# A fused attention, mixing and feed-forward kernel: the feed-forward in 18 tiles of 256 tokens across batch borders instead of 16 tiles of 288

## The chip, the cores and the metric

The program runs on one core of a Trainium2 chip. The metric is the device time of one execution in microseconds (us); of several runs the median counts. The core has five engines that work side by side, each in the order of its own instruction list: TensorE (PE: matrix products; PEld is its weight load), VectorE (DVE), ScalarE (ACT), GpSimd (POOL) and SyncE (SP), which issues the DMAs. TensorE writes its products to PSUM, eight banks of 512 float32 values per partition.

## What is computed

For 8 batches of 576 tokens, with 8 heads of 64 channels:

```python
q_d, k_d, v_d = means of q, k, v over groups of 4 tokens
out_up = repeat(softmax(q_d k_d^T / 8) v_d, 4 tokens)
out_local = softmax(q k^T / 8, keys at a distance under 4) v
x = (out_up + out_local), heads side by side          # 8 x 576 x 512
u = x + (V^T U^T along the tokens) x                  # U: 576 x 32, V: 32 x 576
out = u + relu(u @ w_ch1) @ w_ch2                     # 512 -> 2048 -> 512
```

A pair of heads fills the 128 partitions, so a batch is 4 pairs (`hp` 0 to 3) and the attention is 32 pairs in all. U, V and the two weights come as float64.

## The kernel before

**Feed-forward.** It works on transposed tokens: partitions are channels, columns are tokens. A batch's 576 tokens are cut into two tiles of `TN` = 288, 16 tiles in all. One step is one tile and one of the 16 chunks `fc` of 128 hidden channels, 256 steps in all. `ffn1` (L878) multiplies four channel chunks of u with W1 into one PSUM tile `ps_h`; `ffn2` (L900), three steps later (`LAG`), multiplies the rectified chunk with W2 into four accumulators `acc`, one for each 128 output channels and each in a PSUM bank of its own. To keep precision every operand is split into a high and a low float32r part, and a product is three matmuls (high·high, high·low, low·high): 12 matmuls of 288 columns in `ffn1` and 12 in `ffn2`, with a weight load of 128 columns ahead of each. ACT makes the high part `hH` from `ps_h` (L895), DVE the low part `hL` (L896). At the end of a tile POOL adds uH and uL (L921), DVE adds the accumulator (L924), and a DMA stores 128 channels (L927).

**u.** A tile's u lies in `uH` and `uL` (two buffers each). A head pair of the attention is one of its four channel chunks, so a tile's first step needs all four pairs of its batch. `mix_part` (L816) makes it from the pair's attention output `x_s` in DRAM: `xL` and `Y` are loaded from it, PE multiplies with U (`ps_hu`, L848), then per tile with V (`ps_u`, L863); DVE adds (L866), ACT rounds to `uH` (L869), POOL subtracts for `uL` (L871). Batch 0 takes another way (`early_mix`).

**Attention of a pair.** The first five pairs (batch 0 and pair 0 of batch 1) use `early_global` and `local_blocks`. The others use `late_global` (scores `ps_b`, L719 and L726; transposes `ps_t`, L539; products `ps_a`, L552; result `od`, stored to `up_s`) and `local_attn`, where POOL makes five products `Pt` (L799) and DVE sums them (L804) into `acc`, which goes to `x_s` (L806).

**Weights.** W1 and W2 come in 16 chunks each. `convert` (L335) turns the raw float64 bits into float32 and the two parts: ACT L341, DVE L342, L344, L347 and L349, ACT L351, POOL L354. W2 has its place in SBUF only after the early attention's pool is given back (`late`, L969). The raw chunks and POOL's `Pt` share three buffers (tag `Pt`).

**Order.** Nothing is issued where it is written. Every piece of work is an `op` of a planner (`Plan`, L54) with an engine, an estimated duration, what it reads and writes, and a priority; a simulated run (L95) fixes the order in which each engine's instructions are issued. The attention has 10 times the pair's number as priority, the W2 conversions 20 to 35, and the feed-forward matmuls 1000 plus their step, so they fill what is left of PE. `PH` and `PF` (L222) are the planner's durations for `ffn1`'s 12 matmuls and for three of `ffn2`.

Of the kernel before, what the change touches and what calls it, by code (L numbers as in the profile page):

```python
# [11 lines left out]
F32 = mybir.dt.float32  # L12
# [189 lines left out]
def attn_mix_ffn_kernel(ctx: ExitStack, tc, q, kp, vp, qT, kT, v, U, Ub, V, w1, w2, mask, band, eye, pat, pool, vw, vn, ident, outT):  # L202
# [11 lines left out]
    TN = 288  # L214
    NT = S // TN
    R = V.shape[0] // 4
    MP, MJ = U.shape[0], U.shape[1] // R
    LAG = 3
# [3 lines left out]
    PH, PF = 1.587, 0.398  # L222
# [52 lines left out]
    ident_sb = const.tile([128, 128], F32, name="ident_sb")  # L275
# [15 lines left out]

    band_sb = early_pool.tile([128, NS * KL], BF16, name="band_sb")
# [40 lines left out]
    dma(lambda: nc.sync.dma_start(out=mask_sb, in_=mask), [], ["mask"], 35, 32)  # L333

# [72 lines left out]

    heads = [slice(hh * D, (hh + 1) * D) for hh in range(2)]
# [86 lines left out]
    def late_global(b, hp, up_s, prio):  # L495
# [39 lines left out]
        def t_mm():  # L535
            for hh in range(2):
                for c in range(2):
                    for a in range(2):
                        nc.tensor.transpose(view(pt[hh])[:, c, a * QH:(a + 1) * QH],  # L539
                                            Es[hh]()[:, a, c * QH:(c + 1) * QH], ident_sb[:QH, :QH])  # L540
        op(PE, 0.52, t_mm, ek + ["ident"], pt, prio)
# [13 lines left out]
        od = g([QH, 4, D], "od")  # L555
# [114 lines left out]
    def early_mix(b, hp, x, prio):  # L670
# [14 lines left out]
        for t in range(NT):  # L685
            pu = psum(ps_m, "ps_u", "m:x", 2)
            cuts = [(r, max(t * TN, 128 * r), min((t + 1) * TN, 128 * (r + 1))) for r in range(NS)]
            cuts = [x for x in cuts if x[1] < x[2]]

            def um(t=t, pu=pu, cuts=cuts):  # L690
                tsl = slice(t * TN, (t + 1) * TN)
                nc.tensor.matmul(pu()[:, :TN], stk(), Vst[:, tsl], start=True, stop=False)
                for r, c0, c1 in cuts:
                    nc.tensor.matmul(pu()[:, c0 - t * TN:c1 - t * TN], flat(r), ident_sb[:, c0 - 128 * r:c1 - 128 * r],
                                     start=False, stop=(r == cuts[-1][0]))
            op(PE, pw(prio) * 1.05, um, rd + [(stk, 0), (stk, 1), (stk, 2), "ident", "V0H", "V1H", "V0L", "V1L"], [pu], prio)
            uH, uL = u_of(b, t)
            act(TN, lambda uH=uH, pu=pu: nc.scalar.activation(uH()[:, hp, :], pu()[:, :TN], AF.Copy),
                [pu], [(uH, hp)], prio, 0.05)
            dve(TN, lambda uH=uH, uL=uL, pu=pu: nc.vector.tensor_tensor(  # L700
                out=uL()[:, hp, :], in0=pu()[:, :TN], in1=uH()[:, hp, :].bitcast(F32), op=ALU.subtract),
                [pu, (uH, hp)], [(uL, hp)], prio)
# [106 lines left out]
    u_bufs = {}  # L809

    def u_of(b, t):
        if (b, t) not in u_bufs:
            u_bufs[(b, t)] = (buf(ffn, [128, NDC, TN], F32R, "uH", bufs=2), buf(ffn, [128, NDC, TN], F32R, "uL", bufs=2))
        return u_bufs[(b, t)]

    def mix_part(b, hp, x_s, prio):  # L816
# [21 lines left out]
        dve(576, lambda: nc.vector.transpose(xT(), Y().rearrange("p a d -> p (a d)")), [Y], [(xT, t) for t in range(NT)], prio)  # L838
# [18 lines left out]
        for t in range(NT):  # L857
            tsl = slice(t * TN, (t + 1) * TN)
            pu = psum(ps_m, "ps_u", "m:x", 2)

            def um(tsl=tsl, pu=pu):
                lt = stk().rearrange("p h d -> p (h d)")
                nc.tensor.matmul(pu()[:, :TN], lt, Vst[:, tsl], start=True, stop=True)  # L863
            op(PE, 0.14, um, [(stk, 0), (stk, 1), (stk, 2), "V0H", "V1H", "V0L", "V1L"], [pu], prio)
            uf, ufk = (lambda tsl=tsl: xT()[:, tsl]), (xT, t)
            dve(TN, lambda pu=pu, uf=uf: nc.vector.tensor_tensor(  # L866
                out=uf(), in0=pu()[:, :TN], in1=uf(), op=ALU.add), [pu, ufk], [ufk], prio)
            uH, uL = u_of(b, t)
            act(TN, lambda uH=uH, uf=uf: nc.scalar.activation(uH()[:, hp, :], uf(), AF.Copy),  # L869
                [ufk], [(uH, hp)], prio, 0.1)  # L870
            pool_tt(TN, lambda uH=uH, uL=uL, uf=uf: nc.gpsimd.tensor_tensor(  # L871
                out=uL()[:, hp, :], in0=uf(), in1=uH()[:, hp, :].bitcast(F32), op=ALU.subtract),
                [ufk, (uH, hp)], [(uL, hp)], prio)
# [4 lines left out]
    def ffn1(s, i):  # L878
        b, t, fc = s
        uH, uL = u_of(b, t)  # L880
# [13 lines left out]
        hL = buf(ffn, [128, TN], F32R, "hL", bufs=3)  # L894
# [5 lines left out]
    def ffn2(s, i):  # L900
        b, t, fc = s
# [3 lines left out]
        ac = accs[(b, t)]  # L905

        for e in range(NDC):
            def mm(e=e):
                es = slice(e * 128, (e + 1) * 128)
                for n, (w, hx) in enumerate((("H", hH), ("H", hL), ("L", hH))):  # L910
                    nc.tensor.matmul(ac[e]()[:, :TN], W2[w][:, fc, es], hx(),  # L911
                                     start=(fc == 0 and n == 0), stop=(fc == NFC - 1 and n == 2))
            op(PE, PF, mm, [hH, hL, f"W2_{fc}H", f"W2_{fc}L"], [ac[e]], FILL + i + LAG - 0.5)
        if fc == NFC - 1:
            uH, uL = u_of(b, t)
            for e in range(NDC):
                if e == NDC - 1:
                    o1 = buf(loc, [128, TN], F32, "o1", "o1b", 1)
                else:
                    o1 = buf(ffn, [128, CN], F32, "o1", "cT:o1", 3)  # L920
                pool_tt(TN, lambda e=e, o1=o1: nc.gpsimd.tensor_tensor(  # L921
                    out=o1()[:, :TN], in0=uH()[:, e, :].bitcast(F32), in1=uL()[:, e, :].bitcast(F32), op=ALU.add),
                    [(uH, e), (uL, e), f"W2_{NFC - 1}L"], [o1], FIRST, after=[last_h[i - 1]])
                dve(TN, lambda e=e, o1=o1: nc.vector.tensor_tensor(  # L924
                    out=o1()[:, :TN], in0=ac[e]()[:, :TN], in1=o1()[:, :TN], op=ALU.add),
                    [ac[e], o1], [o1], FIRST)
                dma(lambda e=e, o1=o1: nc.sync.dma_start(  # L927
                    out=outT[e * 128:(e + 1) * 128, b * S + t * TN:b * S + (t + 1) * TN], in_=o1()[:, :TN]),
                    [o1], [], FIRST, 150, lat=0.4)

    steps = [(b, t, fc) for b in range(B) for t in range(NT) for fc in range(NFC)]

# [42 lines left out]
    attention(1, False)  # L975
    for i in range(len(steps) + LAG):
        if i < len(steps):
            b, t, fc = steps[i]
            if t == 0 and fc == 0 and b > 0 and b + 1 < B:
                attention(b + 1)  # L980
# [70 lines left out]
```

## Time and profile before

| | |
|---|---|
| median of 3 runs | 1037.83 us (1037.47 to 1038.42) |
| profiled execution, first to last instruction | 1036.6 us |
| busy share of DVE, POOL, ACT | 51%, 54%, 37% |
| matmuls of the feed-forward | 16 tiles x 16 chunks x 24 = 6144 |
| DMA traffic | 120.30 MB |

The page of the profile has busy times, slices of the span and the chain that ended last; "windows" are busy times in chosen stretches; the timeline lists instructions in order of time, with the idle time before one and what ended it in brackets (start, duration, engine, line, operation, count); a row with x6 stands for six instructions. Matmuls overlap, so a matmul's own duration (0.29 us) is longer than its distance from the next; the distance is what counts.

### The profile page before, as it was taken

What the parts mean: (1) busy time and instruction counts of PE and PEld (TensorE: products, weight loads), DVE (VectorE), ACT (ScalarE), POOL (GpSimd) and SP (SyncE); (2) the same over time, 40 slices, a digit from 0 to 9 for tenths busy, and PEclk for the clock granted to TensorE, in tenths of its full rate; (3) what the DMA queues carried; (4) which work ended last, traced back from release to release, by engine and by line L of the source; (5) the groups of instructions that cost most, each with busy time, mean ns of one, the idle gap of its engine ahead of it and who ended that gap; (6) DMA issues with size and microseconds to landing.
All of it is one profiled execution on the core that took longest, in us unless ns stands there. A gap on an engine that the chain in (4) does not pass through costs nothing.

```text
span 1036.6 us, 26946 instructions
## 1 busy us (share of the span) xinstructions
PE 996.9 (96%) x10831; PEld 975.3 (94%) x10831; DVE 529.8 (51%) x1054; ACT 388.0 (37%) x1234; POOL 557.2 (54%) x567
## 2 busy tenths in 40 slices
PE   6778898999999999999999999999999999999998
PEld 5667888999999999999999999999999999999998
DVE  5997898655554545444475344534652544211111
ACT  3676554442443434443344244423443232111110
POOL 4854568788575656565585638762765625211010
PEclk9896999999999999999999999999999999999999
DMA  8866764753555545545555355624644242000000
GB/s 279 226 172 179 199 186 116 149 138 104 135 137 115 141 113 132 128 86 146 120 137 125 87 132 133 143 75 101 151 116 117 64 113 50 24 1 24 1 24 23
DMA packets 222612, 120.30 MB, mean 116 GB/s; under 512 B 175492, under 2 KB 198456, under 8 KB 222488
## 3 DMA queue, kind: packets, MB, share of 16 engines
q1 hardware_dynamic: 222488, 118.58, 45.5%
q8 instruction: 85, 1.39, 0.6%
q14 instruction: 39, 0.32, 0.1%
HBM read 87.78 MB, written 30.75 MB: 114 GB/s over the span
## 4 chain that ended last, share of the span: by engine, by line
PE 84%; DVE 7%; POOL 3%; issue 2%; DMA 2%; ACT 2%; SPq 0%; DVEq 0%; POOLq 0%; ACTq 0%
PE acc L911 36%; PE ps_h L888 35%; PE ps_a L552 2%; PE ps_b L719 2%; DVE c L347 2%; PE ps_hu L848 1%; DVE c L349 1%; PE ps_t L539 1%; DMA w2r<-in_W 1%; PE ps_b L726 1%; POOL Pt L799 1%; DVE c L342 1%; DVE c L344 1%; PE ps_a L484 1%; PE ps_v L431 1%
## 5 line engine op out<-in xcount | busy, mean ns | idle before, releaser
L911 PE MATMUL acc<-hH,W2H 128*128 128x288 f32 x1024 | 310.5, 303 | 0.0
L896 DVE SCALAR_TENSOR_TENSOR hL<-ps_h,hH 128x288 fp32r<-128x288 f32 x256 | 116.6, 455 | 378.6 <-ACT hH L895 378.0
L888 PE MATMUL ps_h<-uH,W1H 128*128 128x288 f32 x1024 | 304.3, 297 | 4.1 <-DVE hL L896 3.1
L911 PE MATMUL acc<-hH,W2L 128*128 128x288 f32 x1024 | 303.1, 296 | 2.6 <-POOL W2L L354 2.6
L888 PE MATMUL ps_h<-uL,W1H 128*128 128x288 f32 x1024 | 303.4, 296 | 1.2 <-POOL uL L871 1.2
L911 PE MATMUL acc<-hL,W2H 128*128 128x288 f32 x1024 | 302.6, 296 | 0.0
L888 PE MATMUL ps_h<-uH,W1L 128*128 128x288 f32 x1024 | 302.0, 295 | 0.0
L799 POOL TENSOR_TENSOR Pt<-vl,at 128x896 f32<-128x896 f32 (+1 forms) x135 | 233.4, 1809 | 115.1 <-DVE acc L804 61.1
L895 ACT ACTIVATE hH<-ps_h 128x288 fp32r<-128x288 f32 x256 | 105.1, 410 | 433.6 <-PE ps_h L888 433.5
L888 PEld LDWEIGHTS ps_h<-uH,W1H 128*128 128x128 f32 x1024 | 193.5, 189 | 5.4 <-DVE hL L896 3.8
L911 PEld LDWEIGHTS acc<-hH,W2L 128*128 128x128 f32 x1024 | 193.2, 189 | 3.5 <-POOL W2L L354 3.5
L888 PEld LDWEIGHTS ps_h<-uL,W1H 128*128 128x128 f32 x1024 | 193.4, 189 | 1.5 <-POOL uL L871 1.5
L911 PEld LDWEIGHTS acc<-hH,W2H 128*128 128x128 f32 x1024 | 193.3, 189 | 1.1
L888 PEld LDWEIGHTS ps_h<-uH,W1L 128*128 128x128 f32 x1024 | 193.7, 189 | 0.0
L911 PEld LDWEIGHTS acc<-hL,W2H 128*128 128x128 f32 x1024 | 193.7, 189 | 0.0
L804 DVE TENSOR_REDUCE acc<-Pt 128x128 f32<-128x1024 f32 (+1 forms) x135 | 144.7, 1103 | 4.7 <-POOL Pt L799 2.3
L871 POOL TENSOR_TENSOR uL<-xT,uH 128x288 fp32r<-128x288 f32 x56 | 44.1, 811 | 71.3 <-ACT uH L869 71.2
L921 POOL TENSOR_TENSOR o<-uH,uL 128x288 f32<-128x288 f32 x64 | 49.8, 816 | 54.2 <-DMA out_t<-o 54.2
L840 POOL TENSOR_TENSOR xL<-xL,xH 116x640 fp32r<-116x640 f32 x28 | 44.0, 1572 | 64.2 <-ACT xH L839 49.3
L510 POOL TENSOR_TENSOR vr<-vr 72x256 f32<-72x256 f32 x54 | 42.4, 785 | 46.9 <-DMA vr<-in_v 46.8
L793 ACT ACTIVATE Pt<-ul 128x128 f32<-128x128 f32 (+1 forms) x135 | 48.4, 441 | 21.3 <-DVE acc L804 20.0
L744 ACT ACTIVATE se<-ps_b 96x114 f32<-96x114 f32 x108 | 38.5, 357 | 47.1 <-PE ps_b L719 34.1
(129 smaller groups left out, 1106.9 us busy)
## 6 DMA issues: line engine op xcount, KB each, us to landing
vl<-in_vp SPq DMA_DIRECT2D x54, 240.0 KB
out_t<-o SPq DMA_DIRECT2D x64, 144.0 KB
w1r<-in_W SPq DMA_DIRECT2D x16, 512.0 KB
w2r<-in_W SPq DMA_DIRECT2D x16, 512.0 KB
Y<-x_s SPq DMA_DIRECT2D x112, 72.0 KB
gT<-in_kT SPq DMA_DIRECT2D x27, 291.0 KB
xL<-x_s SPq DMA_DIRECT2D x28, 280.0 KB
gq<-in_qT SPq DMA_DIRECT2D x27, 288.0 KB
```

What stands on the lines that cost most here:

```text
L510: pool_tt(256, lambda x=x: nc.gpsimd.tensor_tensor(out=x()[:, :, 0:2, :], in0=x()[:, :, 0:2, :], in1=x()[:, :, 2:4, :], op=ALU.add), [x], ...
L744: act(n * KL, lambda p=ps[hh], se=se, n=n, rows=rows: nc.scalar.activation(se()[rows, 0:n].rearrange("p r k -> p (r k)"), p()[rows, 0:n * ...
L793: act(n * D, lambda n=n, ps=ps, Pt=Pt: nc.scalar.activation(Pt()[:, :n, :, 7], ul()[:, ps, :], AF.Copy), [ul], [(Pt, 1)], prio, 0.16)
L799: nc.gpsimd.tensor_tensor(out=Pt()[:, :n, :, 0:7].rearrange("p s d o -> p o s d"), in0=win, in1=at()[:, ps, :].rearrange("p s o -> p o s") ...
L804: dve(8.5 * n * D, lambda n=n, ps=ps, Pt=Pt: nc.vector.tensor_reduce(out=acc()[:, ps, :], in_=Pt()[:, :n], axis=AX.X, op=ALU.add), [(Pt, 0 ...
L840: pool_tt(640, lambda: nc.gpsimd.tensor_tensor(out=xL(), in0=xL().bitcast(F32), in1=xH().bitcast(F32), op=ALU.subtract), [xL, xH], [xL], prio)
L871: pool_tt(TN, lambda uH=uH, uL=uL, uf=uf: nc.gpsimd.tensor_tensor(out=uL()[:, hp, :], in0=uf(), in1=uH()[:, hp, :].bitcast(F32), op=ALU.su ...
L888: nc.tensor.matmul(ps()[:, :TN], w[:, dc, fs], u()[:, dc, :], start=(n == 0), stop=(n == 3 * NDC - 1))
L895: last_h[i] = act(TN, lambda: nc.scalar.activation(hH(), ps()[:, :TN], AF.Relu), [ps], [hH], FIRST, 0.05)
L896: dve(TN, lambda: nc.vector.scalar_tensor_tensor(hL(), ps()[:, :TN], 0.0, hH().bitcast(F32), op0=ALU.max, op1=ALU.subtract), [ps, hH], [hL ...
L911: nc.tensor.matmul(ac[e]()[:, :TN], W2[w][:, fc, es], hx(), start=(fc == 0 and n == 0), stop=(fc == NFC - 1 and n == 2))
L921: pool_tt(TN, lambda e=e, o1=o1: nc.gpsimd.tensor_tensor(out=o1()[:, :TN], in0=uH()[:, e, :].bitcast(F32), in1=uL()[:, e, :].bitcast(F32), ...
```

## The change

The tokens of all batches are one row of 4608, cut into 18 tiles of 256 (`NG`). A tile may lie across a batch border: `pieces(b)` gives a batch's parts as (tile, first token, count, place in the tile), and `ps_u`, `xT`, `uH` and `uL` are made piece by piece, three for each pair instead of two. A tile's first step waits for every batch that has a part in it (`parts`). Tile 2 holds 64 tokens of batch 0 and 192 of batch 1; tile 4 is the first with batch 2, tile 6 the first with batch 3. `uH` and `uL` have three buffers.

Two output chunks of 256 columns share one PSUM bank, so a tile has two accumulators instead of four, and even and odd tiles have their own. The steps of tiles 0 and 1 alternate chunk by chunk (`first`); the later tiles run one after the other. At a tile's end, POOL, DVE and the store handle two chunks in one instruction, in the last tile DVE and the store one. `ident_sb` moves to the early pool, a 72 x 72 copy `id_late` is loaded for the late pairs, and `od` of the late pairs takes the slot of `gh`. The planner's durations become 1.36 and 0.34.

```diff
-    TN = 288
-    NT = S // TN
+    TN = 256
+    NG = B * S // TN
+    FIRST_TILES = 2
...
-    PH, PF = 1.587, 0.398
+    PH, PF = 1.36, 0.34
...
+            u_bufs[g] = (buf(ffn, [128, NDC, TN], F32R, "uH", bufs=3), buf(ffn, [128, NDC, TN], F32R, "uL", bufs=3))
...
+    def pieces(b):
+        cuts = [b * S] + [x for x in range(0, B * S, TN) if b * S < x < (b + 1) * S] + [(b + 1) * S]
+        return [(x // TN, x - b * S, y - x, x % TN) for x, y in zip(cuts, cuts[1:])]
+
+    parts = {}
+    for b in range(B):
+        for g, _, _, _ in pieces(b):
+            parts.setdefault(g, []).append(b)
...
-        od = g([QH, 4, D], "od")
+        od = buf(glo, [QH, 4, D], F32, "od", "gh:od", 1)
...
-        for t in range(NT):
-            tsl = slice(t * TN, (t + 1) * TN)
+        for g, c, n, off in pieces(b):
...
-        ur = [(uH, c) for c in range(NDC)] + [(uL, c) for c in range(NDC)]
-        op(PE, PH, mm, ur + [f"W1_{fc}H", f"W1_{fc}L"] + ["late"] * (i >= 3), [ps], FILL + i)
+        ur = [(u, c, b) for u in (uH, uL) for c in range(NDC) for b in parts[g]]
+        op(PE, PH, mm, ur + [f"W1_{fc}H", f"W1_{fc}L"] + ["late"] * (i >= HLB), [ps], FILL + i)
...
-            accs[(b, t)] = [psum(ps_acc, f"acc{e}", f"acc{e}", 1) for e in range(NDC)]
+            accs[g] = [psum(ps_acc, f"acc{e}", f"acc{2 * (g % 2) + e}", 1) for e in range(NDC // 2)]
...
+                    nc.tensor.matmul(half(e), W2[w][:, fc, es], hx(), start=(fc == 0 and n == 0 and e % 2 == 0),
+                                     stop=(fc == NFC - 1 and n == 2 and e % 2 == 1))
...
-    steps = [(b, t, fc) for b in range(B) for t in range(NT) for fc in range(NFC)]
+    first = [(g, fc) for fc in range(NFC) for g in range(FIRST_TILES)]
+    steps = first + [(g, fc) for g in range(FIRST_TILES, NG) for fc in range(NFC)]
```

The order on PE shows the first place, the start of layer 2. Before, the first step's twelve products go to four accumulators (numbers in the names are buffers), and the next rows are the next chunk of the same tile:

```order
L911 MATMUL acc_1652<-hH,W2H 128x288
L911 MATMUL acc_1652<-hL,W2H 128x288
L911 MATMUL acc_1652<-hH,W2L 128x288
L911 MATMUL acc_1661<-hH,W2H 128x288
L911 MATMUL acc_1661<-hL,W2H 128x288
L911 MATMUL acc_1661<-hH,W2L 128x288
L911 MATMUL acc_1668<-hH,W2H 128x288
L911 MATMUL acc_1668<-hL,W2H 128x288
L911 MATMUL acc_1668<-hH,W2L 128x288
```

In the changed kernel, at the same place, tile 0's last products of its first chunk (accumulators 1659 and 1664) are followed by tile 1's of the same chunk (1678):

```order
L923 MATMUL acc_1659<-hH,W2H 128x256
L923 MATMUL acc_1659<-hL,W2H 128x256
L923 MATMUL acc_1659<-hH,W2L 128x256
L923 MATMUL acc_1664<-hH,W2H 128x256
L923 MATMUL acc_1664<-hL,W2H 128x256
L923 MATMUL acc_1664<-hH,W2L 128x256
L923 MATMUL acc_1678<-hH,W2H 128x256
L923 MATMUL acc_1678<-hL,W2H 128x256
L923 MATMUL acc_1678<-hH,W2L 128x256
```

So each W2 chunk serves two steps before the next chunk is asked for.

The second place is PE at the first step that needs batch 1. In the changed kernel all 32 steps of tiles 0 and 1 stand before it, layer 2 included; `ps_hu` and `ps_u` are the mixing of batch 1's last pair, and `ps_h` is step 32, the first of tile 2:

```order
L923 MATMUL acc_1685<-hH,W2H 128x256
L923 MATMUL acc_1685<-hL,W2H 128x256
L923 MATMUL acc_1685<-hH,W2L 128x256
L860 MATMUL ps_hu<-xH,Ust 64x128 x5
L860 MATMUL ps_hu<-xL,Ust 64x128 x5
L874 MATMUL ps_u<-Vst,stk 128x192
L874 MATMUL ps_u<-Vst,stk 128x256
L874 MATMUL ps_u<-Vst,stk 128x128
L899 MATMUL ps_h<-uH,W1H 128x256
```

Before, a step and a half of layer 2 still stood behind that `ps_hu`: there it came after 30.5 steps of layer 2, here after 32. In both kernels 32 steps of layer 1 stand ahead, but they are 576 tokens before and 512 now.

The third place is the DMA queue (SP), between the store of that last pair's attention (`x_s<-acc`) and the load of it for the mixing (`xL<-x_s`). Before:

```order
L806 DMA x_s<-acc 128x576
L508 DMA vr<-in_v 72x2x256
L561 DMA up_s<-od 288x1x64 x4
L822 DMA xL<-x_s 112x2x320
L825 DMA xL<-x_s 4x2x320
L833 DMA Y<-x_s 32x18x32 x4
```

And in the changed kernel:

```order
L824 DMA x_s<-acc 128x576
L726 DMA vl<-in_vp 64x960 x2
L587 DMA gq<-in_qT 128x576
L805 DMA ul<-up_s 128x576
L587 DMA gT<-in_kT 128x582
L834 DMA xL<-x_s 112x2x320
L837 DMA xL<-x_s 4x2x320
L845 DMA Y<-x_s 32x18x32 x4
```

The store of another pair's `od`, which waits for PE and DVE, no longer stands between the two; three loads do.

More of the change, by code (lines that the diff above doesn't have):

```diff
@@ L274, in attn_mix_ffn_kernel @@
     nc.scalar.activation(warm, warm, AF.Exp)
-    ident_sb = const.tile([128, 128], F32, name="ident_sb")
+    id_late = const.tile([QH, QH], F32, name="id_late")
     Ust = const.tile([MP, MJ, 2 * R], F32R, name="Ust")
@@ L290, in late_pool @@
         return W2
+    ident_sb = early_pool.tile([128, 128], F32, name="ident_sb")
     band_sb = early_pool.tile([128, NS * KL], BF16, name="band_sb")
@@ L333, in attn_mix_ffn_kernel @@
     dma(lambda: nc.sync.dma_start(out=mask_sb, in_=mask), [], ["mask"], 35, 32)
+    dma(lambda: nc.sync.dma_start(out=id_late, in_=ident[0:QH, 0:QH]), [], ["id_late"], 35, 21)
     def convert(raw, pp, n, hi_out, lo_out, a, wkey, name, prio, gate=(), l0=0):
@@ L914, in ffn2 @@
+            op(PE, PF, mm, [hH, hL, f"W2_{fc}H", f"W2_{fc}L"] + [(ac[e // 2], 0)] * (fc == 0 and e % 2),
+               [(ac[e // 2], e % 2)], FILL + i + LAG - 0.5)
         if fc == NFC - 1:
[L915 to L929, printed above, removed]
@@ L975, in attn_mix_ffn_kernel @@
     attention(1, False)
+    for b in range(2, B):
+        attention(b)
     for i in range(len(steps) + LAG):
         if i < len(steps):
-            b, t, fc = steps[i]
-            if t == 0 and fc == 0 and b > 0 and b + 1 < B:
-                attention(b + 1)
             ffn1(steps[i], i)
```

100 lines of the change are left out of this document (57 added, 43 removed).

## Prediction

> **What bounds the kernel now.** I begin with the page: the busy shares, then the slices of PE.
>
> ```profile
> span 1036.6 us, 26946 instructions
> PE 996.9 (96%) x10831; PEld 975.3 (94%) x10831; DVE 529.8 (51%) x1054; ACT 388.0 (37%) x1234; POOL 557.2 (54%) x567
> PE   6778898999999999999999999999999999999998
> PE 84%; DVE 7%; POOL 3%; issue 2%; DMA 2%; ACT 2%; SPq 0%; DVEq 0%; POOLq 0%; ACTq 0%
> ```
>
> PE is busy nearly all the time except in the first nine of 40 slices (26 us each), and 84% of the chain that ended last is PE. So two things can shorten the kernel: fewer PE microseconds, or less idle PE before about 230 us. The windows say where that idle time lies (columns: stretch, its length, then busy time and count of PE, PEld, DVE, ACT, POOL; granted clock of PE; DMA).
>
> ```profile
> 82.00:102.00 20.00, 16.79 (x285) 15.39 (x289) 16.80 (x30) 12.89 (x35) 10.73 (x10) 0.70 0.74 185
> 102.00:157.00 55.00, 50.01 (x616) 47.44 (x602) 49.17 (x88) 29.48 (x80) 33.16 (x30) 0.95 0.70 193
> 157.00:167.00 10.00, 7.58 (x56) 7.12 (x54) 10.00 (x14) 4.58 (x14) 7.35 (x6) 1.00 0.45 104
> 167.00:229.00 62.00, 60.98 (x666) 60.46 (x667) 38.82 (x77) 28.62 (x99) 50.01 (x48) 0.97 0.58 137
> 229.00:1033.00 804.00, 801.54 (x8204) 795.40 (x8202) 350.30 (x714) 265.11 (x862) 409.97 (x420) 1.00 0.40 97
> ```
>
> From 102 to 167 us PE idles 65 − 57.6 = 7.4 us, with DVE busy 59.2 of 65: this is the conversion of W2. From 167 to 229 us PE is full, DVE is not, and POOL works 50.0 of 62. After 229 us only PE counts. The waits of PE from 82 to 230 us:
>
> ```profile
> PE acc L911 <- POOL W2L L354: 2.6, 4, 1.0
> PE ps_hu L848 <- POOL Ust L354: 2.5, 1, 2.5
> PE ps_h L888 <- DVE hL L896: 2.3, 2, 1.4
> ```
>
> Then the timeline at the first step that needs batch 1 (PE first, then POOL, then the DMA queue SP):
>
> ```profile
> 229.35 0.29 PE L888 MATMUL ps_h<-uH,W1H 128*128 128x288 f32 x1
> ...
> 232.06 0.40 PE L888 MATMUL ps_h<-uL,W1H 128*128 128x288 f32 x1 [1.23 <-POOL uL L871]
> 223.72 1.58 POOL L840 TENSOR_TENSOR xL<-xL,xH 116x640 fp32r<-116x640 f32 x1 [1.94 <-DMA s_s<-se]
> 209.72 0.34 SPq L806 DMA_DIRECT2D x_s<-acc  x1
> ...
> 213.51 3.74 SPq L561 DMA_DIRECT2D up_s<-od  x4
> 217.36 0.47 SPq L822 DMA_DIRECT2D xL<-x_s  x1
> ```
>
> PE has used up batch 0 at 229.35 and, ten matmuls later, waits until 232.06 for batch 1's last pair. So in the kernel before PE's work on batch 0 and the attention of batch 1 end together: **whoever shortens only the first gains nothing before batch 1 is there.**
>
> **The change part by part.** *Split the time at batch 1.* Call R the time from which PE could run without a break. A steady step gives the pace of a 288-column matmul:
>
> ```profile
> 700.85 0.29 PE L888 MATMUL ps_h<-uH,W1H 128*128 128x288 f32 x1
> ...
> 702.44 0.29 PE L911 MATMUL acc<-hH,W2H 128*128 128x288 f32 x1
> ```
>
> Twelve in 1.59 us, 0.1325 each. Ten were done at 232.06, so R = 232.06 − 10 × 0.1325 = 230.7. From there the kernel before takes 1036.6 − 230.7 = 805.9 us: 14 tiles × 384 × 0.1325 = 712.3, and 93.6 for the rest (the PE work of 24 pairs, and 3.8 us from the last matmul, which starts as below, to the end; (93.6 − 3.8) / 24 = 3.7 a pair).
>
> ```profile
> 1032.77 0.29 PE L911 MATMUL acc<-hH,W2L 128*128 128x288 f32 x1
> ```
>
> *Border.* In the changed kernel only 512 tokens instead of 576 can run before R; 16 tiles × 384 = 6144 matmuls of 256 columns come after it, where 5376 of 288 did. The new time is R + 6144 t + 93.6 + extras, so nearly all hangs on t, the pace at 256 columns.
>
> *t.* No row has it. These are nearest: half clock, 128 columns with 64 weight columns, and weight loads of 128 columns back to back.
>
> ```profile
> 92.40:94.80 2.40, 2.40 (x11) 2.37 (x11) 1.67 (x3) 0.86 (x3) 2.24 (x3) 0.50 0.76 141
> 93.87 0.44 PE L888 MATMUL ps_h<-uH,W1L 128*128 128x288 f32 x1
> 94.11 0.44 PE L888 MATMUL ps_h<-uH,W1H 128*128 128x288 f32 x1
> 209.99 0.46 PE L848 MATMUL ps_hu<-xH,Ust 116*64 116x128 f32 x5
> 210.29 0.46 PE L848 MATMUL ps_hu<-xL,Ust 116*64 116x128 f32 x5
> 81.13 0.77 PEld L694 LDWEIGHTS ps_u<-ident_sb,ob 128*128 128x128 f32 x6
> 81.81 0.19 PEld L692 LDWEIGHTS ps_u<-Vst,stk 128*128 128x128 f32 x1
> ```
>
> At a granted clock of 0.50 a matmul of 288 takes 0.240, so the columns alone would take 0.120 at full clock; 0.1325 is 0.0125 more. At 128 columns it is 0.30 / 5 = 0.060, of which the columns are 0.0533: 0.0067 more. Two readings fit. **(a)** The surplus grows with the columns: the line through both points gives 0.060 + 128 × 0.000453 = 0.118 at 256. **(b)** It comes once for each started block of 256 columns, so twice for 288 and once for 256 and 128: 0.1067 + 0.0065 = 0.1132. Weight loads bound it from below: six in 0.68 us, 0.113 each, 0.112 at the least with the rows' rounding. From above 0.1325 is the end, the 288 row itself. By itself (a) is the simpler line. I take (b) by a narrow margin, since the planner's numbers are those of rows wherever a row exists (1.587 / 12 = 0.1323; in the unchanged part 0.6 / 10 = 0.060 for `ps_hu`), and the new 1.36 / 12 and 0.34 / 3 both say 0.1133. That is second-hand, so (a) keeps a large share.
>
> The Trainium skill, "TensorE: Matmul & The Clock Gate", section "Back-to-back issue gap", gives a warm matmul N / 2.4 + 2.5 ns: 122.5 at 288, where this trace has 132.5, and 109.2 at 256. By that rule 6144 t would be 671 us instead of 696, and the time some 1002 us with the waits for batches 2 and 3. The trace disagrees with it at 288.
>
> *The joint tiles.* They ask for a W2 chunk every two steps, so the 2.6 us of waits on W2L and part of the 7.4 us idle go. What is late next is batch 1: 32 steps are 768 × 0.1133 = 87 us of PE, with some five pairs' 3.7 about 105, so from 102 on PE is done near 207 and stands until R. I therefore count no gain from them on PE. They can move R itself, through DVE and ACT queues that no longer stall behind a starved PE, at most by those 7.4 us.
>
> *R.* It is set by POOL and the queue. `Pt` shares its buffers with W2's raw chunks, so it begins when those run out (stretch 157 to 229 us):
>
> ```profile
> L799 POOL TENSOR_TENSOR Pt<-vl,at 128x896 f32<-128x896 f32 (+1 forms) x18 | 31.5, 1824 | 4.2 <-DVE c L349 2.1 <-DMA vl<-in_vp 1.5 <-DVE ri L530 0.5
> L871 POOL TENSOR_TENSOR uL<-xT,uH 128x288 fp32r<-128x288 f32 x6 | 4.7, 804 | 6.0 <-ACT uH L869 6.0
> ```
>
> The 31.5 us of `Pt` stay (17 stand ahead of that load in both orders). On SP the store of `od` held the load of `xL` from 209.72 to 217.36; now three loads stand there, so some 4 us can go. R lies between 222 (that and the conversions' slack) and 231 (nothing gained); I take 227.
>
> *Small parts.* A third `ps_u` matmul for each pair: three times 0.113 for 2 × 0.1325, 0.07 × 24 pairs = 1.7 us on PE. A third `uL`, `uH` and `xT` piece each: POOL has 394 us idle after 229 and hides 24 × 0.8 at most. Fewer and wider `o1` operations and stores, two acc sets by parity, `id_late`, `od` in another slot: beside a full PE, 0; without that cover a tile's `o1` would cost its 1.6 us of POOL once, at the end. There two single-chunk stores remain as before, 0.
>
> *The later borders.* Tile 4 needs batch 2, tile 6 batch 3. Their last `uL` came at (first of each row's two times):
>
> ```profile
> L871 POOL TENSOR_TENSOR uL<-xT,uH x1: 823/823/823, 326.9 to 326.9; 128x288 fp32r<-128x288 f32 x1
> L871 POOL TENSOR_TENSOR uL<-xT,uH x1: 829/829/829, 435.2 to 435.2; 128x288 fp32r<-128x288 f32 x1
> ```
>
> Two tiles with four pairs take 768 × 0.1133 + 4 × 3.7 = 101.8 us. PE reaches tile 4 at 328.8, and batch 2 (moved with R by 3.7) is there at 324; tile 6 at 430.6, batch 3 at 432: 1.5 us of waiting.
>
> *Sum.* 227 + 6144 × 0.1133 (696.1) + 93.6 + 1.7 + 1.5 = 1019.9 of span. The median lies 1037.83 − 1036.6 = 1.2 above the profiled span: **1021 us**, 1.6% faster.
>
> **Rivals.**
> *Slower: the stream sets t.* By (a) 6144 × 0.118 = 725.0: 227 + 725.0 + 93.6 + 1.7 + 1.2 = 1048.5. The place is every feed-forward matmul after R; the columns there grow from 4032 to 4096, and the steady pace no longer pays for the 64 that were pushed behind R. The point is t = (1037.8 − 1.2 − 227 − 95.3) / 6144 = 0.1163; above it the kernel is slower. For it: a straight line through two rows. Against it: the planner's entries.
> *Weight loads alone set t.* At 0.112 it is 6144 × 0.112 = 688.1, and tiles 4 and 6 wait some 4 us for their batches: 227 + 688.1 + 93.6 + 1.7 + 4 + 1.2 = 1016. For it: the loads' rows. Against it: a surplus at both widths that have a row. The page named above would put t lower still, at 0.1092.
> *R moves a lot under (a).* With R at 218, the 7.4 us of idle and the queue's hold both gained, (a) gives 1039: no change.
> *The joint start does what it says and is worth its 7.4 us:* that is R at 223, inside the forecast's range, not another case.
>
> **How the numbers follow.** Forecast 0.55; slower by (a) 0.36; no change 0.05; weight loads alone 0.04. Faster by over 0.2% (2 us, about what a measurement of this kernel can tell) is 0.55 + 0.04, 0.59; same 0.05; slower 0.36. The forecast alone spans 1010 (R 222, t 0.112) to 1026 (R 231). Both signs hold much, so the range goes to (a) with R 231: 1010 to 1052.
>
> **What would show it.** In the profile after: the distance of steady 256-column matmuls, 0.113 or 0.118, decides first. PE should stand before tile 2, waiting for `uL`, for 10 us or more, and hardly wait for W2L; tile 2 should go on at 222 to 231. Short waits or none at tiles 4 and 6. What would make it wrong: R beyond 235, because the third piece of each pair or another order delays batch 1; waits of more than 5 us at a later border; a t between the readings.

## The result, and the profile after

The changed kernel takes 1074.8 us (median of 4 runs, 1067.0 to 1077.3) beside 1037.65 for the kernel before: a ratio of 1.034, 95% interval 1.030 to 1.038. It is 3.4% slower; the forecast was 1021 us, and the time lies above the range's upper end of 1052. The profiled execution spans 1072.8 us, 36.2 more than before.

The page of the changed kernel, the same lines as before, and below them the clock by slices:

```profile
span 1072.8 us, 28628 instructions
PE 1011.2 (94%) x11623; PEld 990.2 (92%) x11623; DVE 534.0 (50%) x1092; ACT 398.8 (37%) x1298; POOL 553.6 (52%) x567
PE   5777898979998999899999999999999999999998
PEclk9786999989999999999999999999999999999999
PE 83%; DVE 6%; DMA 5%; ACT 2%; issue 1%; SPq 1%; POOL 1%; DVEq 0%; ACTq 0%; POOLq 0%
```

PE is busy 14 us longer, and its row now has dents behind the first nine slices: an 8 in the 13th and in the 17th (27 us each). The rest of the 36 us is time in which PE stood. First the pace, from a steady step (start, duration; twelve matmuls of layer 2, then twelve of layer 1):

```profile
701.01 0.28 PE L923 MATMUL acc<-hH,W2H 128*128 128x256 f32 x1
...
702.45 0.28 PE L899 MATMUL ps_h<-uH,W1H 128*128 128x256 f32 x1
...
703.86 0.28 PE L923 MATMUL acc<-hH,W2H 128*128 128x256 f32 x1
```

1.44 / 12 = 0.120 in layer 2, 1.41 / 12 = 0.1175 in layer 1. Over the stretch from 800 us to the end the mean of 2141 distances is 0.1188. Per column that is 0.464 ns, where 0.1324 at 288 columns is 0.460: **a column costs what it did before, within 1%.**

Then where PE stands. The windows round the borders at which a new batch is needed (columns as before):

```profile
216.00:229.00 13.00, 6.91 (x55) 6.33 (x54) 10.28 (x19) 5.43 (x18) 12.22 (x12) 0.85 0.56 135
336.00:346.00 10.00, 6.68 (x47) 6.37 (x46) 9.33 (x16) 3.35 (x11) 7.41 (x11) 0.83 0.51 143
449.00:465.00 16.00, 11.56 (x167) 10.69 (x167) 10.42 (x22) 5.15 (x17) 12.37 (x13) 0.79 0.49 136
465.00:760.00 295.00, 295.00 (x3478) 292.91 (x3477) 138.43 (x294) 112.88 (x393) 165.28 (x177) 1.00 0.48 114
760.00:776.00 16.00, 14.11 (x118) 13.90 (x117) 10.85 (x20) 4.25 (x15) 8.35 (x8) 0.96 0.49 110
```

PE idles 6.1 us before tile 2 (batch 1), 3.3 before tile 4 (batch 2), 4.4 before tile 6 (batch 3) and 1.9 near 770 us; between them it is full. In the four that idle the granted clock falls too, to 0.79 to 0.96. The timeline of PE at tile 2 shows how:

```profile
220.69 0.47 PE L860 MATMUL ps_hu<-xH,Ust 116*64 116x128 f32 x5
224.75 0.52 PE L860 MATMUL ps_hu<-xL,Ust 116*64 116x128 f32 x5 [3.60 <-POOL xL L852]
...
228.82 0.53 PE L899 MATMUL ps_h<-uH,W1H 128*128 128x256 f32 x1
229.15 0.42 PE L899 MATMUL ps_h<-uL,W1H 128*128 128x256 f32 x1
...
231.71 0.40 PE L899 MATMUL ps_h<-uL,W1H 128*128 128x256 f32 x1
```

Tiles 0 and 1 are done at 220.7; tile 2 begins at 228.8, and its first twelve distances from 229.15 on are 0.213 each: after the stand PE runs at half clock for some 3 us (granted clock 0.50 from 229.2 to 231.8).

To put each loss in its place I count the columns of all feed-forward matmuls in order of time; 384 columns are one token's work (24 matmuls for each of 16 chunks). The table has the time, in us from the span's start, at which a token's work was reached (reckoned from the trace's starts), and below it the length of each piece for the two kernels and the experiments that follow:

```
token                        512    640    896   1152   1440   1728   4600
before                     214.9  243.2  296.3  350.2  409.5  468.4 1031.5
changed                    220.7  256.9  310.0  369.7  430.1  499.5 1067.3
later by                     5.8   13.7   13.7   19.5   20.6   31.1   35.8

piece                         512-640 640-896 896-1152 1152-1440 1440-1728 1728-4600
before                          28.3    53.1     53.9      59.3      58.9     563.1
changed                         36.2    53.1     59.7      60.4      69.4     567.8
true planner numbers            36.1    54.4     53.9      59.3      60.3     564.2
single tiles                    43.9    54.8     59.8      60.4      69.5     564.3
both                            38.9    54.1     53.8      59.2      60.2     564.1
kernel before, 72 tokens held   27.1    53.2     50.6      58.9      60.2     561.9
```

Between the borders (tokens 640 to 896, 1152 to 1440) both kernels take the same within 1.1 us. The 36 us are four jumps: 13.7 until batch 1 is under way, 5.8 at tile 4 (token 1024), 10.5 at tile 6 (token 1536), and 4.7 behind (0.6 to 1.2 of it in the experiments at 256 columns too); with the 1.1 between they make the 35.8.

What makes batch 3 late at tile 6 stands in the timeline of ACT:

```profile
442.46 0.38 ACT L906 ACTIVATE hH<-ps_h 128x256 fp32r<-128x256 f32 x1 [2.42 <-PE ps_h L899]
445.31 0.38 ACT L906 ACTIVATE hH<-ps_h 128x256 fp32r<-128x256 f32 x1 [2.47 <-PE ps_h L899]
445.60 1.02 ACT L880 ACTIVATE uH<-xT 128x256 fp32r<-128x256 f32 x3
446.52 0.73 ACT L851 ACTIVATE xH<-xL 116x640 fp32r<-116x640 f32 x1
447.14 0.94 ACT L811 ACTIVATE Pt<-ul 128x128 f32<-128x128 f32 x3
```

ACT does its list in order. Work of the attention (`uH`, `xH`, `Pt`) stands behind two `hH`, and each `hH` waits 2.4 us for the next `ps_h` of the feed-forward. DVE has the same: the add `o` at the end of a tile waits for the tile's last matmul, the attention's sums `acc` stand behind it, and behind these `stk`, for which PE waits (two rows of DVE, then PE):

```profile
448.99 1.41 DVE L938 TENSOR_TENSOR o<-acc,o 128x512 f32<-128x512 f32 x2 [2.15 <-PE acc L923]
450.31 3.46 DVE L822 TENSOR_REDUCE acc<-Pt 128x128 f32<-128x1024 f32 x3
454.23 0.77 PE L874 MATMUL ps_u<-Vst,stk 128*128 128x64 f32 x2 [3.91 <-DVE stk L865]
```

At tile 4 the chain of waits passes through the same place (start, length, what):

```profile
331.15 1.43 PE ps_h L899 x12
...
332.60 0.38 ACT hH L906
332.99 0.26 ACT uH L880
...
333.31 0.51 POOL uL L882
...
335.04 1.52 POOL xL L852
```

A step of the feed-forward ends, ACT makes `hH`, only then `uH`, then POOL can go on to the `xL` that the last pair of batch 2 needs. The last jump has another cause, two lines of SP and DVE:

```profile
760.22 0.57 SPq L776 DMA_DIRECT2D sc<-s_s  x1
```

```profile
767.05 5.62 DVE L788 SCALAR_TENSOR_TENSOR ms<-sc,mask_sb 128x63 f32<-128x63 f32 x1 [0.88 <-DMA sc<-s_s]
```

One load came after 6.7 us, and the DVE instruction on it took 5.62 us where most of its fellows take 0.21 (in every traced run here some of them take 0.6 to 3.5). I found no reason for it; none of the four 256-column experiments in the table and below has this jump (563.7 to 564.3 in the last piece).

### The profile page after: what moved, and what is told of

Read it like the earlier page. It is cut to its first block, busy times and chain, and to the rows that moved or that the text cites. A ratio compares the mean times of both kernels' runs of the same rounds, so it can differ in the third digit from the quotient of the medians.

```text
span 1072.8 us, 28628 instructions
## 1 busy us (share of the span) xinstructions
PE 1011.2 (94%) x11623; PEld 990.2 (92%) x11623; DVE 534.0 (50%) x1092; ACT 398.8 (37%) x1298; POOL 553.6 (52%) x567
## 4 chain that ended last, share of the span: by engine, by line
PE 83%; DVE 6%; DMA 5%; ACT 2%; issue 1%; SPq 1%; POOL 1%; DVEq 0%; ACTq 0%; POOLq 0%
PE ps_h L899 36%; PE acc L923 35%; PE ps_a L570 2%; PE ps_b L737 2%; DMA sc<-s_s 2%; PE ps_hu L860 1%; DMA w2r<-in_W 1%; DMA s_s<-se 1%; DVE acc L822 1%; PE ps_t L557 1%; PE ps_b L744 1%; PE ps_u L874 1%; DVE c L350 1%; PE ps_v L449 1%; DVE c L352 1%
## 5 line engine op out<-in xcount | busy, mean ns | idle before, releaser
L923 PE MATMUL acc<-hH,W2H 128*128 128x256 f32 x1152 | 333.8, 290 | 2.5 <-ACT W2H L354 2.5
L899 PE MATMUL ps_h<-uH,W1H 128*128 128x256 f32 x1152 | 330.5, 287 | 5.5 <-DVE hL L907 5.0
L899 PE MATMUL ps_h<-uH,W1L 128*128 128x256 f32 x1152 | 327.8, 285 | 0.0
L899 PE MATMUL ps_h<-uL,W1H 128*128 128x256 f32 x1152 | 327.5, 284 | 0.0
L923 PE MATMUL acc<-hH,W2L 128*128 128x256 f32 x1152 | 326.2, 283 | 0.8 <-POOL W2L L357 0.8
L923 PE MATMUL acc<-hL,W2H 128*128 128x256 f32 x1152 | 326.4, 283 | 0.0
L907 DVE SCALAR_TENSOR_TENSOR hL<-ps_h,hH 128x256 fp32r<-128x256 f32 x288 | 121.6, 422 | 404.8 <-ACT hH L906 402.4
L817 POOL TENSOR_TENSOR Pt<-vl,at 128x896 f32<-128x896 f32 (+1 forms) x135 | 228.8, 1769 | 106.0 <-DVE acc L822 67.2
L906 ACT ACTIVATE hH<-ps_h 128x256 fp32r<-128x256 f32 x288 | 109.9, 382 | 430.8 <-PE ps_h L899 417.7
L932 POOL TENSOR_TENSOR o<-uH,uL 128x512 f32<-128x512 f32 x36 | 45.7, 1290 | 90.9 <-DVE hL L907 85.5
L882 POOL TENSOR_TENSOR uL<-xT,uH 128x256 fp32r<-128x256 f32 (+3 forms) x84 | 49.4, 604 | 72.9 <-ACT uH L880 72.8
```

Source lines behind the costliest of these rows:

```text
L817: nc.gpsimd.tensor_tensor(out=Pt()[:, :n, :, 0:7].rearrange("p s d o -> p o s d"), in0=win, in1=at()[:, ps, :].rearrange("p s o -> p o s") ...
L882: pool_tt(n, lambda uH=uH, uL=uL, uf=uf, n=n, off=off: nc.gpsimd.tensor_tensor(out=uL()[:, hp, off:off + n], in0=uf(), in1=uH()[:, hp, off ...
L899: nc.tensor.matmul(ps()[:, :TN], w[:, dc, fs], u()[:, dc, :], start=(n == 0), stop=(n == 3 * NDC - 1))
L906: last_h[i] = act(TN, lambda: nc.scalar.activation(hH(), ps()[:, :TN], AF.Relu), [ps], [hH], FIRST, 0.05)
L907: dve(TN, lambda: nc.vector.scalar_tensor_tensor(hL(), ps()[:, :TN], 0.0, hH().bitcast(F32), op0=ALU.max, op1=ALU.subtract), [ps, hH], [hL ...
L923: nc.tensor.matmul(half(e), W2[w][:, fc, es], hx(), start=(fc == 0 and n == 0 and e % 2 == 0), stop=(fc == NFC - 1 and n == 2 and e % 2 == 1))
```

## The experiments

**Two corners of a square, then the others.** Theory A: the planner was told 1.36 and 0.34 (0.1133 a matmul), PE takes 0.1175 and 0.120, so the fixed order puts `hH`, `hL` and `o` too early in the queues, ahead of attention work that could run.

```diff
-    PH, PF = 1.36, 0.34
+    PH, PF = 1.42, 0.36
```

> The changed kernel with PH, PF = 1.42, 0.36, the pace that its own trace shows (12 matmuls at 0.118, 3 at 0.120), in place of 1.36, 0.34. Theory A: the planner's numbers are 4 to 6% too short, so its fixed order gives DVE and POOL work that waits for the feed-forward too early, and the attention's work behind it in those queues comes late; PE then stands at tiles 4 and 6 (3.7 + 1.5 and 5.9 us of stands, and half clock after each) and at 763 us. With the true numbers these stands go: 1048 to 1060 us. Rival B: batches 2 and 3 are late because two tiles of 256 take PE less time than the attention of a batch needs, whatever the order: the stands stay, 1070 to 1078 us. The matmul distance stays 0.118 and 0.120 under both.

Measured: 1064.2 us, ratio to the kernel before 1.025 (1.022 to 1.028). The windows of this run at the same borders:

```profile
336.00:346.00 10.00, 10.00 (x174) 9.81 (x173) 3.90 (x12) 6.18 (x25) 4.88 (x7) 1.00 0.53 134
449.00:465.00 16.00, 16.00 (x146) 16.00 (x144) 6.92 (x13) 7.73 (x28) 13.12 (x14) 1.00 0.65 150
760.00:776.00 16.00, 16.00 (x231) 15.78 (x230) 7.76 (x19) 7.58 (x28) 14.50 (x17) 1.00 0.55 134
```

PE is full and the clock at 1.00 at all three. The pieces 896 to 1152 and 1440 to 1728 fall by 5.8 and 9.1 us to the kernel before's length within 1.4. The gain of the whole is smaller than these 15, because token 640 is reached 9.5 us later: with this order batch 1 comes later.

```diff
-    FIRST_TILES = 2
+    FIRST_TILES = 1
```

> The changed kernel with FIRST_TILES = 1: tiles 0 and 1 one after the other instead of chunk by chunk. If the joint start is worth nothing, since batch 1 sets the end of that stretch: within 4 us of the changed kernel, 1070 to 1079, and PE still stands before tile 2. If the joint start delays batch 1 by its other order on DVE and POOL: tile 2 goes on some 4 us earlier, 1064 to 1070. If it saves the 7.4 us of waits for W2 that the kernel before had: 1079 to 1083.

Measured: 1077.8 us, ratio 1.040 (1.036 to 1.043), beside 1.030 to 1.038 of the changed kernel: the joint start is worth at most a few us. The stands at tiles 4 and 6 stay (59.8 and 69.5 us in the table). With both edits:

> The changed kernel with both FIRST_TILES = 1 and PH, PF = 1.42, 0.36: the fourth corner of a square with the changed kernel (1074.8), the true numbers alone (1064.2) and single tiles alone (1077.8). Theory A (too short planner numbers make the stands at tiles 4 and 6 and behind): no stand of over 1 us at these two borders, from tile 2's first step to the end 822 to 828 us as with the true numbers alone (824.7) and not 836 to 841 as with the short ones; in all 1055 to 1067. Rival: the stands went by the luck of one order: they stay here, 836 us or more from tile 2 on, 1070 or more in all.

Measured: 1067.1 us, ratio 1.026 (1.022 to 1.031). Its windows:

```profile
336.00:352.00 16.00, 16.00 (x231) 15.80 (x229) 6.77 (x18) 7.86 (x29) 10.86 (x12) 1.00 0.62 142
450.00:470.00 20.00, 20.00 (x179) 20.00 (x178) 10.95 (x19) 8.41 (x30) 15.23 (x17) 1.00 0.57 137
```

No stand. In both rows of the square the true numbers take 10.6 or 10.7 us off, and the two pieces at the borders are the same to 0.1 us in the two kernels with short numbers and in the two with true ones. That is no luck of one order: in this tiling the short numbers make these stands.

**The same error put into the kernel before**, 4% short, and its opposite, 2% long:

```diff
-    PH, PF = 1.587, 0.398
+    PH, PF = 1.525, 0.3825
```

> The kernel before (288 columns) with the planner's numbers 4% too short, PH, PF = 1.525, 0.3825. Theory A (a planner that takes the matmuls for faster than they are delays the attention through the queues): slower by 8 to 25 us, with stands of PE at the batch borders near 346 and 463 us and half clock behind them. Rival: the border waits of the changed kernel come from the 256-column tiling alone: within 3 us of 1037.7.

Measured: 1044.7 us, ratio 1.007 (1.005 to 1.010). Slower, but only by 8 us, the least that I had expected, and at another place than I said. The waits of PE from 85 us on, in us, times, longest:

```profile
PE ps_hu L848 <- POOL xL L840: 4.1, 1, 4.1
PE acc L911 <- POOL W2L L354: 3.5, 5, 1.2
```

The long one ends at 227.8 us, before batch 1; at token 640 this kernel is 6.1 us behind, and from 240 us on PE never stands. (At tokens 1152 and 1728 it is 2.7 and 2.9 behind and at the end 7.9: it has put off attention work, which PE does later.) So short numbers alone don't stop PE at the later borders, and whether the 6 us before batch 1 are theirs or come with any other order isn't shown.

What the short numbers do in both tilings shows in the time at which POOL reaches `xL` of batch 2's last pair. At 288 columns, with the kernel's own numbers and then with the short ones:

```profile
319.82 1.56 POOL L840 TENSOR_TENSOR xL<-xL,xH 116x640 fp32r<-116x640 f32 x1 [4.34 <-DMA s_s<-se]
339.09 1.57 POOL L840 TENSOR_TENSOR xL<-xL,xH 116x640 fp32r<-116x640 f32 x1 [4.66 <-DMA vr<-in_v]
```

At 256 columns, with the true numbers and then in the changed kernel:

```profile
323.41 1.57 POOL L852 TENSOR_TENSOR xL<-xL,xH 116x640 fp32r<-116x640 f32 x1 [4.07 <-ACT xH L851]
335.00 1.57 POOL L852 TENSOR_TENSOR xL<-xL,xH 116x640 fp32r<-116x640 f32 x1
```

The short numbers make batch 2 late by 19 us and by 12 us, although with the true numbers at 256 columns batch 1 came 8 us later than in the changed kernel. For batch 3 it is 29 and 17 us. At 288 columns batch 2 is needed at token 1152 and batch 3 at 1728; the changed tiling needs them at 1024 and 1536, 128 and 192 tokens sooner (27 and 40 us by this pace). So at 288 columns with short numbers PE reaches the first step of batch 2 at 350.6, 11 us behind the late `xL`; in the changed kernel it is through with tile 3 at 336.7, as that `xL` ends, and the rest of the mixing is still to come. Both together, less lead and a wrong pace, made those stands.

> The kernel before with planner's numbers 2% too long (1.62, 0.406). With numbers 4% too short it took 1044.7, 8 us more. If only too short numbers hurt, as theory A has it (what waits for the feed-forward is then put late enough in the queues): 1034 to 1042 us. If any other order than the tuned one costs several us, since the end of batch 1 moves with it: 1043 to 1050.

`PH, PF = 1.62, 0.406` gave 1040.75 us, ratio 1.003 (1.0005 to 1.005): at most half a per cent more, inside the time that theory A had, though no gain either.

**The pace by itself.** The widths were put in by tile:

```diff
+        N = WIDTHS[b * NT + t]
+        W = min(N, TN)
...
-                    nc.tensor.matmul(ps()[:, :TN], w[:, dc, fs], u()[:, dc, :],
+                    x0 = min(dc * TN, NDC * TN - N)
+                    nc.tensor.matmul(ps()[:, :N], w[:, dc, fs], u().rearrange("p c n -> p (c n)")[:, x0:x0 + N],
```

> The kernel before, its 16 tiles with feed-forward matmuls of 288, 288, 288, 512, 448, 384, 320, 272, 264, 256, 248, 240, 224, 192, 160 and 128 columns (above 288 in layer 1 alone). Where fewer than 288, the feed-forward of the other columns is left out; above 288 the products of the further columns are not used. Its time means nothing; the distance of steady matmuls does. If the pace is proportional to the columns (0.46 ns each): 0.118 at 256, 0.110 at 240, 0.088 at 192, 0.177 at 384, 0.235 at 512. If weight loads of 128 columns are a floor: it stays at 0.112 for 240 and less. If a surplus comes for each started block of 256 columns, as I predicted: 0.113 at 256, and a jump of 0.007 between 256 and 264.

Three of the widths in the timeline of PE, each from the first of a group to a later one:

```profile
300.26 0.40 PE L892 MATMUL ps_h<-uH,W1H 128*128 128x512 f32 x1
...
301.88 0.39 PE L892 MATMUL ps_h<-uL,W1H 128*128 128x512 f32 x1
...
701.49 0.28 PE L892 MATMUL ps_h<-uH,W1H 128*128 128x256 f32 x1
...
702.78 0.28 PE L892 MATMUL ps_h<-uH,W1L 128*128 128x256 f32 x1
...
796.51 0.28 PE L892 MATMUL ps_h<-uH,W1H 128*128 128x240 f32 x1
...
797.74 0.28 PE L892 MATMUL ps_h<-uH,W1L 128*128 128x240 f32 x1
```

Seven distances in 1.62, eleven in 1.29 and eleven in 1.23 us: 0.231, 0.117 and 0.112. The means of layer 1 for all widths (stands left out):

```
columns  128   160   192   224   240   248   256   264   272   288   320   384   448   512
ns     111.6 111.6 111.4 111.8 112.4 115.3 117.1 121.4 125.1 132.2 146.7 173.3 203.2 230.8
```

Two of the three readings hold, each in its range: up to 240 columns the time stays at 0.112, which fits the loads of 128 weight columns as a floor, and above 248 the time grows by 0.44 ns a column ((230.8 − 132.2) / 224). Nothing jumps between 256 and 264 (4.3 ns for 8 columns, less than the 7 that a new block should have cost): the reading that I chose is false. Layer 2 has 118.6 at 256 here, with each accumulator in its own bank, where the changed kernel with two in a bank has 119.7 by the same count; it is still slower than layer 1, so the shared bank can make at most part of the difference. The next run has the true numbers and the order of the chunks changed:

```diff
-        for e in range(NDC):
+        for e in (0, 2, 1, 3) if g < NG - 1 else range(NDC):
```

> The changed kernel with the true numbers (1.42, 0.36) and layer 2's output chunks in the order 0, 2, 1, 3, so that consecutive groups of three matmuls go to different banks (the last tile as before). If two chunks in one bank cost the 0.002 us by which layer 2 is slower than layer 1 at 256 columns: its distance falls from 0.120 to 0.118, 6 to 7 us less than the 1064.2 of the true numbers alone. If not: 0.119 to 0.120 stays, 1060 to 1068.

Measured: 1063.95 us, ratio 1.023 (1.020 to 1.026) beside 1.025; layer 2's distance stays at 0.120. Writing one bank twice in a row costs nothing that shows. Token 640 is reached at 258.9 here and at 266.4 in the run with the true numbers alone, though no amount of work differs: the arrival of batch 1 moves by several us with another order. This run also meets the objection that the stands went only because batch 1 came late: it reaches token 1440 at 430.0, the changed kernel at 430.1, and it has no stand at tile 6 (60.2 us for the piece), where the changed kernel has one (69.4).

**The edits that also fit 288 columns.** These are the attention of all batches entered at once, the piecewise code, `id_late` and the place of `od`; the third piece of a pair, the joint start, the shared banks, the third u buffer and the wider `o1` operations are not in it.

```diff
-    TN = 256
-    NG = B * S // TN
-    FIRST_TILES = 2
+    EDGES = [288 * g for g in range(17)]
+    FIRST_TILES = 1
...
-            accs[g] = [psum(ps_acc, f"acc{e}", f"acc{2 * (g % 2) + e}", 1) for e in range(NDC // 2)]
+            accs[g] = [psum(ps_acc, f"acc{e}", f"acc{e}", 1) for e in range(NDC)]
```

> All the changed kernel's other edits at 16 tiles of 288 in order: piecewise u, all batches' attention entered at once, id_late, od in gh's slot; four accumulators in banks of their own, u in two buffers, durations 1.587 and 0.398. If the loss is the width's (64 tokens moved behind batch 1 at an unchanged pace per column, numbers of the planner that the pace doesn't have): 1034 to 1042 us, the kernel before. If one of the other edits costs: 1045 or more.

Measured: 1053.0 us, ratio 1.013 (1.010 to 1.016), which spoke for the rival. But this kernel had three o1 buffers for four chunks, PE waited for `o`, and the last store was late. With the fourth buffer:

> The run with all other edits at 288 columns once more, with the kernel before's fourth o1 buffer, which that run lacked (PE waited 2.8 us for an accumulator that DVE's o had not read, and the last store came 2.1 us later). If the missing buffer was its loss: 1037 to 1045 us, no wait of acc on o. If the other edits cost it: 1050 to 1055 as there (1053.0).

Measured: 1039.75 us, ratio 1.002 (1.000 to 1.004), and no wait of `acc` on `o`. These edits cost 2 us or nothing (0 to 4 by the interval). With the fourth buffer the time is 13 us shorter; the traces differ by 5.4 us before token 640 and by 9.6 behind token 1728, so not all of it need be the buffer's.

**Tokens pushed behind batch 1.** Held back in the kernel before, nothing else changed:

```diff
+        if NT * NFC - 4 <= i < NT * NFC:
+            ur += [(x, c) for x in u_of(1, 0) for c in range(NDC)]
```

> The kernel before (16 tiles of 288, its own numbers) with one thing added: the last four steps of tile 1, the work of 72 tokens, also wait for all of batch 1's first u tile. If tokens moved behind the end of batch 1 cost their full time, as I now hold of the changed kernel's 64: 4 x 24 x 0.1325 = 12.7 us more, 1046 to 1053 us, with the 512th token near the kernel before's 214.7 us and the 640th some 10 to 13 us behind its 243.0. If PE fills the gap with other work, or batch 1 comes earlier for it: within 4 us of 1037.3.

Measured: 1048.8 us, ratio 1.009 (1.006 to 1.012), 9.9 us more. (Token 512 is itself among the 72 held, so its expected 214.7 was my slip: it is reached at 231.6.) The 640th token comes 15.5 us late, and two of those are half clock (20 matmuls at 0.24), as the first held step shows:

```profile
228.37 0.82 PE L863 MATMUL ps_u<-Vst,stk 128*128 128x288 f32 x2 [1.32 <-DVE stk L853]
228.99 0.45 PE L888 MATMUL ps_h<-uH,W1H 128*128 128x288 f32 x1
229.23 0.45 PE L888 MATMUL ps_h<-uL,W1H 128*128 128x288 f32 x1
```

The distance is 0.24. Afterwards the kernel wins back 3.3 us at the next border, where it takes 50.6 us in place of 53.9. So work moved behind batch 1 costs most of its time: 9.9 us in all, 2 of them half clock, where 4 steps are 12.7. The reverse, the push undone in the changed tiling:

```diff
+    EDGES = [0, 288] + [576 + 252 * g for g in range(17)]
```

> Batch 0 in two tiles of 288, the other 4032 tokens in 16 tiles of 252 across the batch borders, with the rest of the changed kernel's edits, single tiles in order, four accumulators in banks of their own, two u buffers, and durations of the planner by the widths run (0.0055 + 0.00044 per column: 0.1164 at 252). So 576 tokens stand before batch 1 again, and only the pushing of 64 tokens behind it is undone. If that push is worth its 64 x 384 columns' time (11 us) in the 1064 to 1067 of the 256-column kernels with true numbers: 16 x 384 x 0.117 = 719 us of matmuls behind batch 1 where the kernel before has 713, and 2 to 5 more for pieces and waits: 1044 to 1053 us, and the 640th token is done within 5 us of the kernel before (243.0). If the push costs nothing: 1060 or more.

Measured: 1141.75 us, ratio 1.099 (1.094 to 1.103): the expected time failed, by a mistake in the experiment. Only two u buffers fitted, and a batch of 576 tokens lies in three or four tiles of 252, so a batch's mixing had to wait until tiles of the one before were done (waits of PE over the span):

```profile
PE ps_hu L863 <- ACT xH L854: 29.5, 6, 7.9
PE ps_hu L863 <- POOL xL L855: 12.6, 7, 3.4
```

So it doesn't settle the price of the push. What it has before that bites is token 640 at 249.2, between the kernel before's 243.2 and the changed one's 256.9, but 6 us behind the former where I had said 5 at most.

**An attempt at something faster.** Wider tiles where the widths run has them cheaper by the column:

```diff
+    EDGES = [288 * g for g in range(8)] + [2304 + 384 * g for g in range(7)]
...
-    LAG, HLB = 3, 3
+    LAG, HLB = 2, 2
```

> The same with 384 columns in the last four batches (eight tiles of 288, then six of 384; to make room LAG = 2 with three hH and two hL buffers and one se buffer). By the widths run a matmul of 384 takes 0.1733 us: 6 x 384 x 0.1733 = 399.3 us in place of 8 x 384 x 0.1325 = 407.0, so 7.7 us less: 1026 to 1033 us, if nothing else waits. Rival: the shorter distance between the layers or the single se buffer makes PE wait for hL or the attention: 1037 or more.

Measured: 1063.5 us, ratio 1.024 (1.020 to 1.027). Two terms failed. The pace, from one group of layer 1 to the next of layer 2:

```profile
1001.11 0.34 PE L903 MATMUL ps_h<-uH,W1H 128*128 128x384 f32 x1
...
1003.23 0.33 PE L927 MATMUL acc<-hH,W2H 128*128 128x384 f32 x1
```

2.12 / 12 = 0.177 in layer 1, 0.460 ns a column as at 288, not the 0.1733 of the widths run, whose layer 1 read other columns of u (whether that is the reason, no run shows). Layer 2 has 0.1734, the expected pace, so this term cost 6 × 192 × 0.0036 = 4.1 us. And the second wide tile crosses a border: PE stood 11.4 us between 660 and 680 us, before a tile that needs batch 5 after 384 tokens of batch 4 instead of 576. No version here beats the kernel before.

## Why the prediction was wrong

- **What bounds the kernel** was right: PE's pace behind batch 1, and the arrival of batch 1 before it.
- **t is the step that failed.** I took reading (b), a surplus for each started block of 256 columns, "by a narrow margin", because the planner's entries said 0.1133. The trace has 0.1188, reading (a)'s 0.118 and a little; 6144 × 0.0055 = 33.8 us. The entries were no measurement, and they did harm of their own, as the square shows. (The Trainium skill's rule in "TensorE: Matmul & The Clock Gate", section "Back-to-back issue gap", which that section gives for an isolated matmul, is 109.2 ns at 256 columns; this trace disagrees with it at both widths, with 118.8 and 132.4 ns.)
- **R**: tile 2 begins at 228.8, and 15 matmuls at 0.213 cost 15 × 0.0945 = 1.4 more, so R is 230.2, inside 222 to 231, 3.2 above the 227 taken and nearly the 230.7 of the kernel before. The load of `xL` was issued some 4 us sooner (213.38 for 217.36), as forecast, but POOL came to `xL` at 223.16 for 223.72, since two `Pt` and an `o` stood ahead of it: that part of the gain was not there. That PE would be done near 207 was wrong by 14 us (it was at 220.7): layer 2 began only at 111.5, 8 us later than in the kernel before.
- **The 64 tokens** behind R were in the sum (6144 matmuls in place of 5376). Of the 13.7 us of the first jump they are 64 × 384 × 0.464 ns = 11.4 and the half clock 1.4, an estimate from this trace that the held-token run bears out in the main.
- **The later borders** failed in size: 1.5 us forecast. I took batch 2 and 3 to arrive when they did before, moved with R, so that the last pair's first `uL` would be there at 324 and 432. In the changed order its ACT, DVE and POOL work stands behind `hH` and `o` of a slower feed-forward, and that `uL` began at 342.1 and 455.8 (with the true numbers at 333.0 and 440.4). The rest of the sum, 1072.8 − (1019.9 + 33.8 + 3.2) = 15.9, is what remains for these stands with the half clock behind them and the 4.7 behind, most of it the stray stand near 770 us; the table has 21.0 for these three jumps, counted from the kernel before, so the sum's other terms are 3.6 too large together. The true numbers took 15 us off the two pieces.
- **The small parts** at or near nothing: nothing speaks against it, but only some were tried. Those that fit 288 columns cost 2 us or less together; the order of the chunks in a bank showed nothing. No run has the third piece, the third u buffer or the wider `o1` operations alone.
- **The joint start at no gain**: not settled finer than some 3 us (1077.8 against 1074.8, 1067.1 against 1064.2).
- **The rival "the stream sets t"** was right in its mechanism, at 1048.5 us; it lacked the stands (15.9 and the 1.5 that only the forecast had), R's 3.2 and 0.0008 a matmul (4.9 in all): 1048.5 + 17.4 + 3.2 + 4.9 = 1074.0, beside 1074.8.

What stays open: why the arrival of batch 1 moves between token 640 at 257 and 268 us with orders that differ little; why layer 1 and layer 2 differ by 0.002 us at 256 columns, hardly at 288, and the other way round by 0.0036 at 384; and what makes single DVE instructions such as the one at 767 us long.

## What to carry to other kernels

An entry in a planner's table is a claim about the chip, not a measurement: measure the pace of the new shape alone before you re-plan with it. Where several engines work through fixed lists, an operation told too short does harm elsewhere: what waits for it stands ahead of what could run, and the more so the less lead the next stage has. A tile that crosses a batch border asks for the next batch sooner; count that lead in tokens and us for each border, the first above all, where what was pushed behind it cost most of its time here.

## What the runs showed that I had not expected

- At 256 columns the twelve matmuls of a layer-1 group have two paces that hold for the whole group. Most have 0.1178; 8 groups of some 280 have 0.1134, and a few lie between. One of the 8 in the changed kernel:

```profile
119.79 0.28 PE L899 MATMUL ps_h<-uH,W1H 128*128 128x256 f32 x1
...
121.15 0.28 PE L923 MATMUL acc<-hH,W2H 128*128 128x256 f32 x1
```

  1.36 / 12 = 0.1133, the planner's very number. Were every group like it, 6912 matmuls would take 38 us less (6912 × 0.0055). I found no cause, and layer 2 never shows it.
- The stands of PE at tiles 2, 4 and 6 of the changed kernel were each followed by 2 to 3 us at a granted clock near 0.50 (0.213 a matmul), which adds 1.0 to 1.4 us to each; in the held-token run it was 4.8 us (0.240 a matmul at 288 columns) and 2.2.
- Below about 245 columns a narrower matmul saves nothing: 0.112 us at 240 as at 128.
